# Twenty attention pairs' state and score products: from whole-array and bf16-split products to fp32 quarters in two PSUM banks

## The chip, the cores and the metric

The kernel runs on one core of a Trainium2 chip. The metric is device time in microseconds of one execution, the median over runs; lower is better. TensorE is called PE here, VectorE DVE, ScalarE ACT, GpSimd POOL and SyncE SP, as in the profile.

## The reference, cut to what matters

Three layers follow each other: a linear attention with a per-channel decay, a gated feed-forward layer behind an RMS norm, and a second feed-forward layer with a squared ReLU. The change touches only the first.

```python
# B, H, S, D = 4, 8, 768, 48
for t in range(S):
    cur = einsum('bhd,bhe->bhde', u * k[t], v[t])
    y[t] = einsum('bhd,bhde->bhe', r[t], state + cur)
    state = w[t][..., None] * state + einsum('bhd,bhe->bhde', k[t], v[t])
x = y as (B*S, H*D) = (3072, 384)
x = (silu(xn @ w_gate) * (xn @ w_val)) @ w_out        # xn = x/rms(x)*g, d_ff 1536
out = (s * relu(x @ w_in)**2 + b) @ w_out2            # d_ff 2048
```

## The kernel before, in words

**Attention.** The 768 steps are cut into 6 chunks of 128 steps, and with the 4 batches that gives 24 pairs (`jb` 0 to 23, in the text pairs 1 to 24; `jb // 4` is the chunk, `jb % 4` the batch). `attention(jb, t)` (L322) does one pair for all 8 heads: running products of the decays on DVE (L340, L347), r and k scaled by them (L352, L353), then on PE the scores k against r (`scores`, L383 to L393: 64x64 quarters of each head pair, the two heads p = 0, 1 of a head pair on partitions 0 to 47 and 64 to 111, each into a PSUM bank of its own) with the transposes of k, the copy and causal masking of the scores into the tiles `a` (L410, L411), and then `sums` (L432). `sums` adds into one PSUM bank y what the state gives (L437: 8 products of 112 rows by 64 columns against 96 columns of the state, from pair 5 on, since the first four pairs have no state yet) and what the scores give (L444 or L449), and calls `news` (L454, L457), which makes the increment of the state. An fp32 product of the source stands as two records in the trace, a bf16 or an fp32r one as one.

**Two forms of the score product.** For pairs 1 to 12 (`fine` false) each head is one fp32 product of 128x128 scores against 48 columns of v (L444, 8 products). For pairs 13 to 24 (`FINE = 12`) the scores and v are each split into three bf16 parts (`split_a` L506, `split_v` L516: ACT copies to bf16, DVE or POOL subtracts), and six part products per head run in bf16 (L449, 48 products).

**Room.** PSUM banks 5, 6 and 7 go round among the uses of pairs 5 to 24 (`bank`, L314), in program order: two for the scores, one for the transposes of k, one for y, one for the state's increment, one for the turned x. The bf16 parts of the scores lie in the same room as the tiles `pat` of the weight conversion: `open_fine` (L494) hands the room over after the first layer's weights are converted, `close_fine` (L500) hands it back at the start of the last chunk.

**After sums.** DVE adds u's part, `av`, to y into `ys` (L476); ACT and POOL form the norm, PE turns the row block (L532), ACT and DVE split it into fp32r high and low parts (L539, L540), and the feed-forward layers use them.

**Feed-forward layers.** `mm_in` (L607) and `mm_out` (L590 to L592) make three fp32r products of 128x128 against up to 512 columns for each block, in place of a full fp32 one. Weights come as 64-bit words and are converted on DVE, ACT and POOL (L569 to L581).

**Checks.** Behind the attention, at low priority, DVE reads all decays and weights again and tests their range (`check_decay` L711, `check_weight` L721); 64 loads feed them. At the end a flag chooses a slow path, which is not taken here.

**Order.** Each piece of work is an `op` with a due time, engines and a cost. `Plan.issue` (L129) simulates the five engines and writes down each engine's list: an idle engine takes the ready op with the smallest due time. The due time orders and doesn't hold back. The lists are fixed at build time, so on the chip every engine runs its list in order, and a wrong cost shows as a wait at the head of a list. A DMA is an op of SP with the cost `nbytes / 350e3 + 0.06`, and what it feeds is reckoned ready 2.0 us after that (`PASS["sp"]`). While the first feed-forward steps lack work, the plan fills PE with products of zeros (`idle`, L792).

Of the kernel before, what the change touches and what calls it, by code (L numbers as in the profile page):

```python
# [10 lines left out]
F32 = mybir.dt.float32  # L11
# [12 lines left out]
C = 128  # L24
# [28 lines left out]
FINE, EARLY, NU, NM, NZ, LENT = 12, 12, 4, 4, 8, 6  # L53
SIX = (0, 0), (0, 1), (0, 2), (1, 0), (1, 1), (2, 0)
# [46 lines left out]
class Plan:  # L101
# [27 lines left out]
    def issue(self):  # L129
# [14 lines left out]
        while events:  # L144
# [12 lines left out]
            for e, queue in ready.items():  # L157
                while queue and free[e] <= now:
# [46 lines left out]
def body(ctx: ExitStack, tc: tile.TileContext, rkw, nat, w1, w2, cst, out):  # L205
# [16 lines left out]
    RAW, PAT, SA = [None] * 2, [None] * 2, [None] * 2  # L222
    SV, = tiles(1, "sv", [128, 3, H, D], BF16)
# [55 lines left out]
    def split_room(fine):  # L279
        for i in range(2):  # L280
            if fine:
                SA[i] = sb.tile([128, 3, HP, C], BF16, name=f"sa{i}", tag=f"small{i}")
            else:
                RAW[i] = sb.tile([128, 2 * DM], I64, name=f"raw{i}", tag=f"big{i}")
                PAT[i] = sb.tile([128, 2 * DM], U32, name=f"pat{i}", tag=f"small{i}")

    split_room(False)

# [33 lines left out]
    def attention(jb, t):  # L322
# [36 lines left out]
        fine = jb >= FINE  # L359
# [63 lines left out]
        if fine:  # L423
            split_a(t, A)
            split_v(td, v, n, q)

        i = bank(jb)
        y = PS[i][:, 0:DM].rearrange("p (h d) -> p h d", h=H)
        iu = None if last else bank(jb)
        U = None if last else PS[iu][:RW, 0:HP * D].rearrange("p (h d) -> p h d", h=HP)  # L430

        def sums(e):  # L432
            first = True
            if jb >= B:
                for h in range(HP):
                    for c0 in (0, 64):
                        nc.tensor.matmul(y[c0:c0 + 64, 2 * h:2 * h + 2, :], r[:, h, c0:c0 + 64], ST[b][:, h],  # L437
                                         start=h == 0, stop=False, skip_group_check=True)
                first = False
            for p in range(2):  # L440
                for h in range(HP):
                    end = p == 1 and h == HP - 1
                    if not fine:
                        nc.tensor.matmul(y[:, 2 * h + p, :], AT[A[p]][:, h, :], v[:, 2 * h + p, :],  # L444
                                         start=first, stop=end, skip_group_check=True)
                        first = False
                    else:
# [16 lines left out]
        reads = [(n, p, x) for n in ("sa", "sv") for p in range(2) for x in range(3)] if fine else [("a", s) for s in A]  # L464
        if jb < NU:
            op(t, {"pe": 1.8 + 0.9 * (jb >= B)}, sums, reads + [("v", q)] + [("r", q), ("st", b, 0), ("st", b, 1)] * (jb >= B),
               [("ps", i)])
# [25 lines left out]

    def open_fine(t):  # L494
        keys = [(n, i) for n in ("raw", "pat") for i in range(2)]
        keys += [("sa", i, x) for i in range(2) for x in range(3)]

        op(t, {"pool": 0.0}, lambda e: split_room(True), (), keys, False)

    def close_fine(t):  # L500
        keys = [(n, i) for n in ("raw", "pat") for i in range(2)]
        keys += [("sa", i, x) for i in range(2) for x in range(3)]
        op(t, {"pool": 0.0}, lambda e: split_room(False), (), keys, False)


    def split_a(t, A):  # L506
        for p in range(2):
            s, N = A[p], HP * C
            for x in range(2):
                op(t, {"act": act(N)}, lambda e, s=s, x=x, p=p: nc.scalar.activation(  # L510
                    SA[p][:, x], AT[s], AF.Copy), [("a", s)], [("sa", p, x)])
                op(t, {"dve": vec2(N), "pool": gps(N)}, lambda e, s=s, x=x, p=p: E[e].tensor_tensor(
                    SA[p][:, 2] if x else AT[s], AT[s], SA[p][:, x], ALU.subtract),
                    [("sa", p, x)], [("a", s)] + [("sa", p, 2)] * x)

    def split_v(t, v, n, q):  # L516
        rest, src = n[1], v
        for x in range(2):
# [489 lines left out]
```

## Time and profile before

| | us |
|---|---|
| median of 3 runs | 1000.93 (1000.35 to 1003.07) |
| the profiled execution | 1002.0 |
| its span, first to last instruction | 1000.3 |
| PE busy in the span | 982.5 |
| DVE busy | 669.5 |
| ACT busy | 419.1 |
| POOL busy | 207.6 |

"Busy" of PE counts each product from start to end, and products overlap, so a busy PE need not be at its peak; the distance from one block's start to the next block's start says what a block takes. The chain of waits goes back from the last instruction to what released each step, so what lies on it set the end.

### The profile page before, as it was taken

What the parts mean: (1) busy time and instruction counts of PE and PEld (TensorE: products, weight loads), DVE (VectorE), ACT (ScalarE), POOL (GpSimd) and SP (SyncE); (2) the same over time, 40 slices, a digit from 0 to 9 for tenths busy, and PEclk for the clock granted to TensorE, in tenths of its full rate; (3) what the DMA queues carried; (4) which work ended last, traced back from release to release, by engine and by line L of the source; (5) the groups of instructions that cost most, each with busy time, mean ns of one, the idle gap of its engine ahead of it and who ended that gap; (6) DMA issues with size and microseconds to landing.
All of it is one profiled execution on the core that took longest, in us unless ns stands there. A gap on an engine that the chain in (4) does not pass through costs nothing.

```text
span 1000.3 us, 16015 instructions
## 1 busy us (share of the span) xinstructions
PE 982.5 (98%) x6344; PEld 812.8 (81%) x6346; DVE 669.5 (67%) x1111; ACT 419.1 (42%) x861; POOL 207.6 (21%) x255
## 2 busy tenths in 40 slices
PE   8999999999999999999999999999999999999997
PEld 5887998888888888888888888887778888888886
DVE  7998997456665665554589789999993433433432
ACT  4645642344454444454434334343343433433333
POOL 3202300124445454454303431000000000000000
PEclk9999999999999999999999999999999999999998
DMA  8554552122222221121294566676650000000001
GB/s 243 188 165 132 183 181 82 57 74 62 83 75 59 74 76 53 52 75 43 81 278 150 176 205 203 210 240 226 219 191 1 22 11 1 31 1 1 32 1 35
DMA packets 45569, 106.82 MB, mean 107 GB/s; under 512 B 4016, under 2 KB 19632, under 8 KB 45488
## 3 DMA queue, kind: packets, MB, share of 16 engines
q1 hardware_dynamic: 45488, 105.73, 33.4%
q8 instruction: 51, 0.84, 0.3%
q14 instruction: 30, 0.25, 0.1%
HBM read 94.71 MB, written 11.01 MB: 106 GB/s over the span
## 4 chain that ended last, share of the span: by engine, by line
PE 83%; DVE 9%; DMA 4%; ACT 3%; issue 1%; SPq 0%; ACTq 0%; DVEq 0%
PE b L607 43%; PE b L590 10%; PE b L591 10%; PE b L592 10%; DMA raw<-in_w 3%; PE b L389 2%; PE b L449 2%; PE b L444 1%; PE b L437 1%; PE b L393 1%; PE b L457 1%; DMA out_t<-o 1%; DVE pat L575 1%; DVE hl L681 1%; DVE pat L741 1%
## 5 line engine op out<-in xcount | busy, mean ns | idle before, releaser
L607 PE MATMUL b<-xh,w 128*128 128x512 f32 (+1 forms) x1566 | 486.3, 375 | 1.0 <-DVE sg L303 0.8
L607 PEld LDWEIGHTS b<-xh,w 128*128 128x128 f32 x1566 | 287.8, 188 | 54.2 <-DVE sg L303 1.4
L607 PE MATMUL b<-xl,w 128*128 128x512 f32 (+1 forms) x783 | 292.0, 373 | 0.5 <-DVE xl L540 0.5
L590 PE MATMUL b<-hh,w 128*128 128x512 f32 (+1 forms) x537 | 206.4, 384 | 1.9 <-ACT in L642 0.7
L591 PE MATMUL b<-hl,w 128*128 128x512 f32 (+1 forms) x537 | 203.4, 379 | 1.4 <-DVE hl L681 1.1
L592 PE MATMUL b<-hh,w 128*128 128x512 f32 (+1 forms) x537 | 202.4, 377 | 0.0
L306 ACT ACTIVATE sg<-b 128x512 f32<-128x512 f32 (+1 forms) x179 | 102.0, 570 | 222.7 <-PE b L607 221.2
L607 PEld LDWEIGHTS b<-xl,w 128*128 128x128 f32 x783 | 147.7, 189 | 26.0 <-DVE xl L540 0.7
L678 DVE SCALAR_TENSOR_TENSOR sg<-sg,cs,b 128x512 f32<-128x512 f32 (+1 forms) x97 | 71.8, 740 | 99.2 <-ACT sg L306 98.9
L590 PEld LDWEIGHTS b<-hh,w 128*128 128x128 f32 x537 | 101.1, 188 | 21.9 <-ACT hh L306 1.3
L591 PEld LDWEIGHTS b<-hl,w 128*128 128x128 f32 x537 | 101.2, 188 | 21.2 <-DVE hl L681 2.9
L592 PEld LDWEIGHTS b<-hh,w 128*128 128x128 f32 x537 | 101.1, 188 | 18.3
L306 ACT ACTIVATE hh<-sg,cs 128x512 fp32r<-128x512 f32 (+1 forms) x97 | 69.7, 719 | 88.2 <-DVE sg L678 82.7
L681 DVE SCALAR_TENSOR_TENSOR hl<-sg,cs,hh 128x512 fp32r<-128x512 f32 (+1 forms) x97 | 73.0, 752 | 48.8 <-ACT hh L306 48.8
L306 ACT ACTIVATE hh<-sg 128x512 fp32r<-128x512 f32 (+1 forms) x82 | 47.5, 579 | 110.4 <-DVE sg L303 110.1
L303 DVE TENSOR_TENSOR sg<-b,sg 128x512 f32<-128x512 f32 (+1 forms) x82 | 51.1, 623 | 50.7 <-PE b L607 49.2
L303 DVE TENSOR_TENSOR hl<-sg,hh 128x512 fp32r<-128x512 f32 (+1 forms) x82 | 54.1, 660 | 13.9 <-ACT hh L306 13.6
L581 POOL TENSOR_TENSOR w<-pat,w 128x384 fp32r<-128x384 f32 x28 | 34.2, 1238 | 67.7 <-ACT w L579 64.8
L411 POOL TENSOR_SCALAR_AFFINE_SELECT a<-a 128x512 f32<-128x512 f32 x38 | 29.9, 807 | 78.9 <-ACT a L306 78.9
L579 ACT ACTIVATE w<-pat 128x384 fp32r<-128x384 f32 x68 | 33.1, 520 | 30.0 <-DVE pat L575 27.9
L573 DVE SCALAR_TENSOR_TENSOR pat<-raw,pat 128x768 uint32<-128x768 uint32 (+1 forms) x40 | 36.8, 925 | 0.0
L540 DVE SCALAR_TENSOR_TENSOR xl<-b,cs,xh 128x128 fp32r<-128x128 f32 x72 | 20.8, 344 | 22.4 <-ACT xh L306 22.4
(132 smaller groups left out, 1005.8 us busy)
## 6 DMA issues: line engine op xcount, KB each, us to landing
raw<-in_w SPq DMA_DIRECT2D x56, 768.0 KB, 4.6
in<-in_rkw SPq DMA_DIRECT2D x24, 448.0 KB, 4.5
raw<-in_w SPq DMA_DIRECT2D x24, 384.0 KB, 3.6
n<-in_nat SPq DMA_DIRECT2D x18, 384.0 KB, 3.2
in<-in_rkw SPq DMA_DIRECT2D x24, 226.6 KB, 2.6
x2d<-o SPq DMA_DIRECT2D x21, 256.0 KB, 2.5
a<-in_rkw SPq DMA_DIRECT2D x24, 224.0 KB, 3.7
v<-in_nat SPq DMA_DIRECT2D x24, 192.0 KB, 3.5
```

What stands on the lines that cost most here:

```text
L303: op(when, {e: cost[e] for e in engines}, lambda e: E[e].tensor_tensor(dst, a, b, f), reads, writes, port)
L306: op(when, {"act": act(n)}, lambda e: nc.scalar.activation(dst, src, func, **kw), reads, writes)
L411: op(t, {"pool": 0.60}, lambda e, s=A[p]: nc.gpsimd.affine_select(out=AT[s], in_=AT[s], compare_op=ALU.is_gt, fill=0.0, base=0, pattern=[[ ...
L573: op(t, {"dve": vec2(N)}, lambda e, word=word, pat=pat: nc.vector.scalar_tensor_tensor(pat(), word(1), 0xC0000000, pat(), ALU.bitwise_and, ...
L579: op(t, {"act": act(DM)}, lambda e, c=c, s=s, pat=pat: nc.scalar.activation(W[s][:, 0], pat(c).bitcast(F32), AF.Copy), [("pat", pi)], [("w ...
L581: op(t, {"dve": vec2(DM)} if ph == 0 else {"dve": vec2(DM), "pool": gps(DM)}, lambda e, c=c, s=s, pat=pat: E[e].tensor_tensor(W[s][:, 1], ...
L590: nc.tensor.matmul(dst, wt[:, 0, cols], xh, start=first, stop=False, skip_group_check=True)
L591: nc.tensor.matmul(dst, wt[:, 0, cols], xl, start=False, stop=False, skip_group_check=True)
L592: nc.tensor.matmul(dst, wt[:, 1, cols], xh, start=False, stop=last, skip_group_check=True)
L607: nc.tensor.matmul(dst, W[s][:, w, kk * 128:(kk + 1) * 128], xx[x][:, kk, sl], start=first and j == kk == 0, stop=last and kk == KD - 1 an ...
L678: op(t, {"dve": vec2(n)}, lambda e: nc.vector.scalar_tensor_tensor(sg, sg, s_col, p, ALU.mult, ALU.mult), [("ps", i)], [("sg", q)], False)
L681: op(t, {"dve": vec2(n)}, lambda e: nc.vector.scalar_tensor_tensor(hl, sg, b_col, hh.bitcast(F32), ALU.add, ALU.subtract), [("sg", q), ("h ...
```

## The change

For pairs 5 to 24 the products of state and scores are made in fp32 on quarters of the array (64 rows by 64 columns), what the two row halves give going into two PSUM banks, Y[0] and Y[1]. The state product becomes 16 products of 48 rows by 64 columns against 48 columns, and the score product 32 products of 64 by 64 against 48 columns. A second add on DVE, of the second bank, follows the first. The bf16 splits, their tiles and the handing over of their room go; pairs 1 to 4 keep their form. The plan's cost for `sums` is now 1.5 and 0.6 us. It also reckons at least 0.47 us for a DMA on SP, and 6 us more for the landing of the checks' loads.

```diff
-FINE, EARLY, NU, NM, NZ, LENT = 12, 12, 4, 4, 8, 6
-SIX = (0, 0), (0, 1), (0, 2), (1, 0), (1, 1), (2, 0)
+EARLY, NU, NM, NZ, LENT = 12, 4, 4, 8, 6
...
@@ Plan.issue
-                        begin[k] = max(begin[k], free[e] + self.PASS[e])
+                        begin[k] = max(begin[k], free[e] + self.PASS[e] + (self.ops[i][3] if e == "sp" else 0.0))
...
-    RAW, PAT, SA = [None] * 2, [None] * 2, [None] * 2
-    SV, = tiles(1, "sv", [128, 3, H, D], BF16)
+    RAW, PAT = tiles(2, "raw", [128, 2 * DM], I64), tiles(2, "pat", [128, 2 * DM], U32)
+    zero, = tiles(1, "zero", [128, NB], BF16)
...
-    def dma(when, dst, src, nbytes, reads=(), writes=()):
-        op(when, {"sp": nbytes / 350e3 + 0.06}, lambda e: nc.sync.dma_start(
-            out=dst() if callable(dst) else dst, in_=src), reads, writes)
+    def dma(when, dst, src, nbytes, reads=(), writes=(), land=0.0):
+        op(when, {"sp": max(0.47, nbytes / 350e3 + 0.06)}, lambda e: nc.sync.dma_start(
+            out=dst, in_=src), reads, writes, land)
...
@@ attention
-        if fine:
-            split_a(t, A)
-            split_v(td, v, n, q)
-
-        i = bank(jb)
-        y = PS[i][:, 0:DM].rearrange("p (h d) -> p h d", h=H)
+        iy = [bank(jb) for _ in range(1 + (jb >= B))]
+        i = iy[0]
+        Y = [PS[i][:, 0:DM].rearrange("p (h d) -> p h d", h=H) for i in iy]
         iu = None if last else bank(jb)
         U = None if last else PS[iu][:RW, 0:HP * D].rearrange("p (h d) -> p h d", h=HP)
 
+        def quarters(e):
+            for h in range(HP):
+                for c0 in (0, 64):
+                    for p in range(2):
+                        nc.tensor.matmul(Y[p][c0:c0 + 64, 2 * h + p, :], r[64 * p:64 * p + D, h, c0:c0 + 64],
+                                         ST[b][64 * p:64 * p + D, h, p, :], start=h == 0, stop=False,
+                                         skip_group_check=True)
+            for j in range(H):
+                h, p = divmod(j, 2)
+                for c0 in (0, 64):
+                    for z in range(2):
+                        rows = slice(64 * z, 64 * z + 64)
+                        nc.tensor.matmul(Y[z][c0:c0 + 64, j, :], AT[A[p]][rows, h, c0:c0 + 64], v[rows, j, :],
+                                         start=False, stop=j == H - 1, skip_group_check=True)
+
         def sums(e):
-            first = True
             if jb >= B:
-                for h in range(HP):
-                    for c0 in (0, 64):
-                        nc.tensor.matmul(y[c0:c0 + 64, 2 * h:2 * h + 2, :], r[:, h, c0:c0 + 64], ST[b][:, h],
-                                         start=h == 0, stop=False, skip_group_check=True)
-                first = False
-            for p in range(2):
-                for h in range(HP):
-                    end = p == 1 and h == HP - 1
-                    if not fine:
-                        nc.tensor.matmul(y[:, 2 * h + p, :], AT[A[p]][:, h, :], v[:, 2 * h + p, :],
-                                         start=first, stop=end, skip_group_check=True)
-                        first = False
-                    else:
-                        for x, z in SIX:
-                            nc.tensor.matmul(y[:, 2 * h + p, :], SA[p][:, x, h, :], SV[:, z, 2 * h + p, :],
-                                             start=False, stop=end and x == 2, skip_group_check=True)
+                quarters(e)
+            else:
...
-            op(t, {"pe": (1.3 if fine else 1.8) + 0.9 + 0.6 * (not last)}, sums,
+            op(t, {"pe": 1.5 + 0.6 * (not last)}, sums,
                reads + [("r", q), ("v", q), ("st", b, 0), ("st", b, 1)] + [tk] * (not last),
-               [("ps", i)] + ([] if last else [("ps", iu)]))
+               [("ps", i) for i in iy] + ([] if last else [("ps", iu)]))
             ys, yk = YS[q], ("ys", q)
-            tt(t, DVE, DM, ys, PS[i][:, 0:DM], AV[q].rearrange("p h d -> p (h d)"), ALU.add,
-               [("ps", i), ("av", q)], [yk])
+            tt(t, DVE, DM, ys, PS[iy[0]][:, 0:DM], AV[q].rearrange("p h d -> p (h d)"), ALU.add,
+               [("ps", iy[0]), ("av", q)], [yk])
+            tt(t, DVE, DM, ys, PS[iy[1]][:, 0:DM], ys, ALU.add, [("ps", iy[1])], [yk])
...
-    def open_fine(t):
...
-    def close_fine(t):
...
-    def split_a(t, A):
...
-    def split_v(t, v, n, q):
...
@@ check_decay
-        dma(t, w, rkw[jb, :, 0:HP * WL].rearrange("p (h t) -> p h t", h=HP)[:, :, 1:], RW * HP * C * 4, (), [("a", s)])
+        dma(t, w, rkw[jb, :, 0:HP * WL].rearrange("p (h t) -> p h t", h=HP)[:, :, 1:], RW * HP * C * 4, (), [("a", s)], 6.0)
...
@@ check_weight
-        dma(t, raw, (w1, w2)[ph][f, :, o * DM:o * DM + n], 128 * n * 8, (), [("raw", ri)])
+        dma(t, raw, (w1, w2)[ph][f, :, o * DM:o * DM + n], 128 * n * 8, (), [("raw", ri)], 6.0)
...
-    later(beg[0, 1] + 7 * 5.5, open_fine, beg[0, 1] + 7 * 5.5)
...
-    later(last, close_fine, last)
```

Left out of the diff are the bodies of the functions that go, the lines of pairs 1 to 4, and a few in which `raw` and `pat` are named directly instead of by a function.

## Rows read from the trace of the kernel before

**Rows 1.** Page: busy time and share of the span, instructions; the granted clock in 40 slices.
```profile
PE 982.5 (98%) x6344; PEld 812.8 (81%) x6346; DVE 669.5 (67%) x1111; ACT 419.1 (42%) x861; POOL 207.6 (21%) x255
...
PEclk9999999999999999999999999999999999999998
```

**Rows 2.** Page: chain that ended last, shares by engine.
```profile
PE 83%; DVE 9%; DMA 4%; ACT 3%; issue 1%; SPq 0%; ACTq 0%; DVEq 0%
```

**Rows 3.** Chain in order of time, 60 to 152 us: start, length, what.
```profile
59.71 0.33 DVE sg L303
...
76.39 0.56 DVE ys L303
...
91.48 0.53 DVE ys L303
...
108.21 0.46 DVE ys L303
...
120.09 0.81 PE b L437 x16
120.91 1.92 PE b L444 x16
...
134.91 0.34 DVE sg L303
...
135.30 2.42 PE b L607 x18
```

**Rows 4.** Stretches of 25 us: busy (x instructions) by engine, clock, DMA share, GB/s.
```profile
150.00:175.00 25.00, 25.00 (x119) 20.95 (x118) 17.81 (x32) 7.12 (x14) 1.25 (x3) 1.00 0.27 82
...
500.00:525.00 25.00, 25.00 (x167) 20.68 (x166) 21.37 (x36) 8.09 (x17) 1.59 (x2) 1.00 0.94 276
...
625.00:650.00 25.00, 25.00 (x112) 20.70 (x111) 24.86 (x52) 7.53 (x12) 0.00 (x0) 1.00 0.65 212
...
675.00:700.00 25.00, 24.47 (x107) 19.60 (x106) 24.31 (x47) 7.37 (x12) 0.00 (x0) 1.00 0.66 228
700.00:725.00 25.00, 24.29 (x106) 19.56 (x105) 23.51 (x41) 7.78 (x12) 0.00 (x0) 1.00 0.65 218
725.00:750.00 25.00, 24.66 (x108) 19.86 (x108) 23.27 (x45) 10.72 (x18) 0.00 (x0) 1.00 0.53 193
```

**Rows 5.** Waits, 660 to 760 us: who waited for whom: us, times, longest.
```profile
DVE pat L733 <- DMA raw<-in_w: 3.5, 3, 1.5
...
PE b L591 <- DVE hl L681: 1.1, 3, 0.5
```

**Rows 6.** Timeline of PE, pair 12: start, us, what (records in a row merged).
```profile
233.33 0.88 PE L437 MATMUL b<-st,in 112*64 112x96 f32 x16
234.14 1.99 PE L444 MATMUL b<-v,a 128*128 128x48 f32 x16
236.05 0.67 PE L457 MATMUL b<-v,kt 128*64 128x48 f32 x16
236.65 0.51 PE L590 MATMUL b<-hh,w 128*128 128x512 f32 x1
```

**Rows 7.** Timeline of PE, pair 15, a pair with bf16 splits.
```profile
291.50 0.39 PE L590 MATMUL b<-hh,w 128*128 128x512 f32 x1
...
293.54 0.39 PE L607 MATMUL b<-xh,w 128*128 128x512 f32 x1
...
295.67 0.88 PE L437 MATMUL b<-st,in 112*64 112x96 f32 x16
296.48 1.37 PE L449 MATMUL b<-sv,sa 128*128 128x48 bf16 x48
297.78 0.67 PE L457 MATMUL b<-v,kt 128*64 128x48 f32 x16
298.38 0.50 PE L590 MATMUL b<-hh,w 128*128 128x512 f32 x1
```

**Rows 8.** Timeline of PE, the quartered scores of pair 15.
```profile
285.89 1.10 PE L389 MATMUL b<-in 48*64 48x128 f32 x32
286.92 0.60 PE L393 MATMUL b<-cs,in 112*128 112x112 f32 x4
```

**Rows 9.** Line L389 alone in a stretch of 30 ns: PE and PEld busy (x records).
```profile
285.89:285.92 0.03, 0.03 (x4) 0.03 (x4) 1.00 0.00 0
```

**Rows 10.** Groups by line and shape: busy us, mean ns, idle before.
```profile
L510 ACT ACTIVATE sa<-a 128x512 bf16<-128x512 f32 x48 | 28.9, 632 | 6.9 <-POOL a L411 3.6 <-POOL a L512 1.9 <-DVE a L512 1.0
...
L303 DVE TENSOR_TENSOR ys<-b,av 128x384 f32<-128x384 f32 x20 | 11.1, 555 | 19.6 <-PE b L449 16.7 <-PE b L444 2.3 <-ACT av L376 0.5
```

More of the change, by code (lines that the diff above doesn't have):

```diff
@@ L277, in body @@
     planned = [True]
-    def split_room(fine):
-        for i in range(2):
-            if fine:
-                SA[i] = sb.tile([128, 3, HP, C], BF16, name=f"sa{i}", tag=f"small{i}")
-            else:
-                RAW[i] = sb.tile([128, 2 * DM], I64, name=f"raw{i}", tag=f"big{i}")
-                PAT[i] = sb.tile([128, 2 * DM], U32, name=f"pat{i}", tag=f"small{i}")
-    split_room(False)
     def op(when, engines, fn, reads=(), writes=(), port=True):
@@ L358, in attention @@
         td = t + TD
-        fine = jb >= FINE
         i2 = [bank(jb), bank(jb)]
@@ L432, in sums @@
         def sums(e):
-            first = True
             if jb >= B:
-                for h in range(HP):
-                    for c0 in (0, 64):
-                        nc.tensor.matmul(y[c0:c0 + 64, 2 * h:2 * h + 2, :], r[:, h, c0:c0 + 64], ST[b][:, h],
-                                         start=h == 0, stop=False, skip_group_check=True)
-                first = False
-            for p in range(2):
-                for h in range(HP):
-                    end = p == 1 and h == HP - 1
-                    if not fine:
-                        nc.tensor.matmul(y[:, 2 * h + p, :], AT[A[p]][:, h, :], v[:, 2 * h + p, :],
-                                         start=first, stop=end, skip_group_check=True)
-                        first = False
-                    else:
-                        for x, z in SIX:
-                            nc.tensor.matmul(y[:, 2 * h + p, :], SA[p][:, x, h, :], SV[:, z, 2 * h + p, :],
-                                             start=False, stop=end and x == 2, skip_group_check=True)
+                quarters(e)
+            else:
+                for j in range(H):
+                    p, h = divmod(j, HP)
+                    nc.tensor.matmul(Y[0][:, 2 * h + p, :], AT[A[p]][:, h, :], v[:, 2 * h + p, :],
+                                     start=j == 0, stop=j == H - 1, skip_group_check=True)
@@ L462, in more @@
                              skip_group_check=True)
-        reads = [(n, p, x) for n in ("sa", "sv") for p in range(2) for x in range(3)] if fine else [("a", s) for s in A]
+        reads = [("a", s) for s in A]
         if jb < NU:
-            op(t, {"pe": 1.8 + 0.9 * (jb >= B)}, sums, reads + [("v", q)] + [("r", q), ("st", b, 0), ("st", b, 1)] * (jb >= B),
-               [("ps", i)])
+            op(t, {"pe": 1.8}, sums, reads + [("v", q)], [("ps", i)])
             op(t, {"pe": 0.7}, more, [("av", q), "cs"], [("ps", i)])
@@ L492, in attention @@
         cp(t, DM + 170, xg, ys, [yk, ("rs", q)], [xk], scale=rs[:, 0:1])
-    def open_fine(t):
-        keys = [(n, i) for n in ("raw", "pat") for i in range(2)]
-        keys += [("sa", i, x) for i in range(2) for x in range(3)]
-        op(t, {"pool": 0.0}, lambda e: split_room(True), (), keys, False)
-    def close_fine(t):
-        keys = [(n, i) for n in ("raw", "pat") for i in range(2)]
-        keys += [("sa", i, x) for i in range(2) for x in range(3)]
-        op(t, {"pool": 0.0}, lambda e: split_room(False), (), keys, False)
-    def split_a(t, A):
[L507 to L514, printed above, removed]
-    def split_v(t, v, n, q):
-        rest, src = n[1], v
-        for x in range(2):
-            keys = [("sv", p, x) for p in range(2)]
-            cp(t, DM, SV[:, x], src, [("v", q), ("n", 0)], keys)
-            tt(t, BOTH, DM, SV[:, 2] if x else rest, src, SV[:, x], ALU.subtract,
-               keys + [("v", q)], [("n", 0)] + [("sv", p, 2) for p in range(2)] * x)
-            src = rest
     def attention_x(jb, t):
@@ L549, in weights @@
             N = n * DM
-            def raw(ri=ri, N=N):
-                return RAW[ri][:, 0:N]
+            raw = RAW[ri][:, 0:N]
             def word(i, raw=raw):
-                return raw().bitcast(U32).rearrange("p (n two) -> p n two", two=2)[:, :, i]
+                return raw.bitcast(U32).rearrange("p (n two) -> p n two", two=2)[:, :, i]
             def pat(c=slice(0, N), pi=pi):
@@ L767, in start @@
         dma(60, cs[:, CU:], cst[:, CU:], 128 * DM * 4, (), ["cu"])
-        zero = SV.rearrange("p a h d -> p (a h d)")[:, 0:NB]
         def consts(e):
```

12 lines of the change are left out of this document (4 added, 8 removed).

## The prediction

> **What bounds the kernel now.** I read the page's busy times first: PE 98% of the span, DVE 67%, at a granted clock of nine tenths or more in every slice but the last [rows 1]. That a busy PE is also what sets the end is for the chain of waits to say: PE holds 83% of it, DVE 9%, DMA 4% [rows 2]. The next view is the chain in order of time, to see where the other engines hold it. From 59.7 to 111 us it runs on DVE in the main, from there to 127 us on PE, then on DVE again up to the product "sg" at 134.91, and from 135.30 on PE [rows 3]. The stretches of 25 us agree: from 150 to 675 us PE's column is full, with one product after the other, each 227 ns behind the last (nine between 291.50 and 293.54 [rows 7]), and between 675 and 750 us it shows 107, 106 and 108 products where a full stretch has 112 [rows 4]. So time taken from PE counts where PE holds the chain: nearly all of it after 135 us, none of it while DVE holds it.
>
> **The products, from 135 us on.** Pairs 9 to 24 lie there. A block's price is the distance from its start to the start of the next block. In pair 12, the old form without splits, the state takes 234.14 - 233.33 = 0.81 us and the scores 236.05 - 234.14 = 1.91, together 2.72 [rows 6]. In pair 15, with splits, it is 0.81 and 1.30, together 2.11 [rows 7].
>
> The new block has 16 state and 32 score products, each two records: 96 records, 24 for each quarter of the array. No such block stands in the trace, but three of its kind do. Each of them sends 8 records through its slowest part: the increment (L457, weights 64 wide) takes 298.38 - 297.78 = 0.60 us [rows 7], the state (96 columns) 0.81, the quartered scores (the quarters with 128 columns) 286.92 - 285.89 = 1.03 [rows 8]. From one to the next a column costs 0.21 / (8 x 32) = 0.82 and 0.22 / (8 x 32) = 0.86 ns, say 0.84, and a fixed 0.60 - 8 x 64 x 0.84 = 0.17 us is left. The new records stream 48 columns but load 64, so I count 64: 24 x 64 x 0.84 = 1.29, plus 0.17 = 1.46 us. The old scores, 16 records of 128, come to 1.72 by this and took 1.91, so the fixed part grows by about 0.02 to 0.03 per 8 records; for 16 more I add 0.06 and take **1.52 us**. As the upper end all of L457's time is put on its records, 0.60 / 8 x 24 = 1.80. All this needs four quarters at work at once. The quartered scores show it: four of their records are at work within 30 ns of the first start [rows 9].
>
> Pairs 9 to 12 save 4 x (2.72 - 1.52) = 4.8 us, pairs 13 to 24 save 12 x (2.11 - 1.52) = 7.1, together **11.9 us**; with 1.46 it is 12.8, with 1.80 it is 7.4.
>
> **Pairs 5 to 8.** They lie around 76 to 123 us, where DVE holds the chain at the add into ys of pairs 5, 6 and 7 (76.39, 91.48, 108.21) and PE at pair 8 (120.09) [rows 3]. The second add puts another DVE instruction there, 0.555 us by the mean of the first [rows 10]; on the chain the first adds hold 0.56, 0.53 and 0.46, so three more are +1.5. Pair 8's products give back 1.20. Net I take **+0.3 us**. Ends: four adds and no gain, +2.2; all four blocks gained as later ones are, -4.8.
>
> **Second adds and banks of later pairs.** The add of pairs 9 to 24 costs nothing on the path: DVE is busy 17.8 of 25 us at 150 us [rows 4], and what it feeds is due a chunk later. If that cover were gone, each would cost 0.5 us. The seventh claim on three banks makes the next pair's scores wait for readers that are through long before, pairs being (295.67 - 233.33) / 3 = 21 us apart on PE [rows 6, 7]. Price nothing.
>
> **Splits removed.** 48 ACT copies of 632 ns [rows 10], and as many subtractions on DVE and POOL, go; they ran beside a full PE, so their going frees engines and no time. What is late next there is still PE. The two hand-overs of room cost POOL nothing; without them the second layer's weights can be loaded before the last chunk starts. The stretch 500 to 525, with DMA at 0.94, had a full PE anyway [rows 4]: nothing.
>
> **Costs in the plan.** Only order can change by them. The floor of 0.47 us for a DMA touches a few small ones. The 6 us more for the checks' loads move DVE's check instructions back in its list. Today DVE waits at its head for such a load (L733, 3.5 us in three waits), while "hl", which PE needs, is queued behind it; L591 waits for that [rows 5]. SP's own list holds the same 64 loads, and nothing that PE needs waits on it there. The most to be had is the 3 x 112 - 321 = 15 products missing, 15 x 0.227 = 3.4 us [rows 4]; as lower end a re-drawn list loses as much. I take **-2.0**, between the 1.1 that PE shows as waits for hl alone and 3.4.
>
> **Sum.** -11.9 + 0.3 - 2.0 = -13.6 us. Against the profiled execution, 1002.0, it gives 988.4; the median of the runs is 1.1 lower, so **987.3 us**. With all ends: 1000.9 - 12.8 - 4.8 - 3.4 = 979.9, and 1000.9 - 7.4 + 2.2 + 3.4 = 999.1; the upper ends are unlikely to meet, so 996.
>
> **A rule against it.** The bf16 block starts its 48 records at 1.30 / 48 = 27 ns each [rows 7]; the new block needs 16 ns. The Trainium skill, "TensorE: Matmul & The Clock Gate", section "Wait — 56ns, not 53.3ns?", says that starts never come closer than about 25 ns, however few the columns. Taken for the whole array, an estimate from it is 96 x 25 = 2.4 us for a block, and the sum would be 12 x 0.29 - 4 x 0.32 = +2.2 us in place of -11.9. The four records within 30 ns [rows 9] speak against it across quarters.
>
> **Rivals.** (1) Pace of issue: 96 records can't follow each other faster than the bf16 ones do. For it: no block of the trace keeps up 16 ns for long. Against it: rows 9. At 27 ns a block takes 2.60 us: 12 x 0.49 - 4 x 0.12 = +5.4, and with +0.3 and -2.0 the time is 1004.6, slower. It decides from 23.5 ns a record on, where a block takes (4 x 2.72 + 12 x 2.11) / 16 = 2.26 us. (2) The change doesn't do what it says, the two row halves taking turns: 48 x 64 x 0.84 + 0.17 = 2.75 us a block, +7.8, 1007. Against it: the scores' four quarters took 1.03 us, the time of one quarter's 8 records. (3) The head pays as well: PE has other work at hand while DVE is late, and pairs 5 to 8 give up to 4.8 us: 982. Against it: the chain's DVE stretches. (4) DVE's crowded stretch takes it back. From 600 to 750 us DVE is nearly full, and PE comes to it 12 us earlier. If each of the ten stretches from 500 to 750 lost what the worst one loses (6 products, 1.4 us), it is 13.6 lost in place of 3.4: 1000.9 - 11.9 + 0.3 + 10.2 = 999.5, no change; half of it is 993. Against it: the checks can go on into 750 us and later.
>
> **How the numbers follow.** The forecast 0.62, (3) 0.13, (4) 0.13 of which 0.05 near no change, (1) 0.08, (2) 0.04. Less than 0.3%, 3 us, is about what a measurement can't tell from no change. Faster: 0.62 + 0.13 + 0.08 and a little of (1), 0.84; same 0.06; slower 0.10. The range 980 to 996 holds the forecast, (3) and half of (4), and leaves out (1), (2) and the rest of (4), 0.17.
>
> **What would show it.** Right: from the state's first record to the increment's (L457) some 1.5 us in every pair from 5 on, 96 records, no L449, no splits; PE full from about 135 us; the whole chain from there moved up by 12 us at 525; 112 products in the stretches that had 107, 106 and 108. Wrong: a block above 2.2 us (rivals 1, 2); the block short but PE's stretches with gaps (4); a second add of ys on the chain after 150 us; the head shorter than before (3).

## The result, and the profile after

The changed kernel takes 990.77 us (median of 4 runs, 989.73 to 992.74), the kernel before 1001.17 in the same comparison (4 runs, 1000.35 to 1003.07). The ratio is 0.9896, with a 95% interval of 0.9873 to 0.9919: 10.4 us less. That is faster, as forecast, inside the range, and 3.5 us above the 987.3 forecast. The profiled execution took 989.75 us, with a span of 988.0.

The page of the changed kernel: busy time by engine, and the chain that ended last, by engine.

```profile
PE 967.2 (98%) x7242; PEld 800.9 (81%) x7242; DVE 644.0 (65%) x1084; ACT 379.5 (38%) x789; POOL 173.3 (18%) x230
...
PE 89%; DVE 5%; ACT 2%; DMA 2%; issue 1%; POOL 0%; DVEq 0%; ACTq 0%; POOLq 0%
```

PE is busy for 15.3 us less than before [rows 1], though it has 898 records more. Its share of the chain rose from 83% to 89%, DVE's fell from 9% to 5% [rows 2]. The next view is the timeline of PE at pair 9 (start, us, what; records in a row merged), the counterpart of [rows 6] and [rows 7].

```profile
178.87 0.68 PE L421 MATMUL b<-st,in 48*64 48x48 f32 x32
179.37 1.11 PE L429 MATMUL b<-v,a 64*64 64x48 f32 x64
180.42 0.67 PE L446 MATMUL b<-v,kt 128*64 128x48 f32 x16
181.01 0.50 PE L547 MATMUL b<-hh,w 128*128 128x512 f32 x1
```

L421 are the state's quarters, L429 the scores', L446 the increment. From the state's first record to the increment's is 180.42 - 178.87 = 1.55 us, where the old block took 2.72 or, with splits, 2.11. In the last four pairs there is no increment, and the old block took less, as the timeline of PE before the change shows at pair 21:

```profile
434.97 0.88 PE L437 MATMUL b<-st,in 112*64 112x96 f32 x16
435.78 1.37 PE L449 MATMUL b<-sv,sa 128*128 128x48 bf16 x48
437.00 0.48 PE L590 MATMUL b<-hh,w 128*128 128x512 f32 x1
```

That is 437.00 - 434.97 = 2.03 us. The sixteen blocks of pairs 9 to 24 give 4 x 1.17 + 8 x 0.56 + 4 x 0.48 = 11.1 us, or 11.2 with the durations unrounded. The stretches show what became of it (busy and count of PE, PEld, DVE, ACT, POOL, then clock, DMA share, GB/s; the last line is a closer look at 10 us).

```profile
75.00:100.00 25.00, 19.17 (x244) 15.49 (x244) 21.39 (x36) 13.41 (x43) 9.36 (x14) 0.93 0.46 129
...
150.00:175.00 25.00, 25.00 (x129) 21.39 (x128) 23.93 (x41) 7.83 (x16) 1.01 (x3) 1.00 0.60 179
...
200.00:225.00 25.00, 25.00 (x335) 20.39 (x326) 17.44 (x32) 9.75 (x23) 10.33 (x16) 1.00 0.31 90
...
575.00:600.00 25.00, 24.31 (x106) 19.49 (x105) 22.37 (x28) 12.29 (x24) 10.49 (x9) 1.00 0.65 216
...
650.00:675.00 25.00, 24.77 (x109) 20.14 (x108) 18.08 (x34) 10.50 (x17) 0.00 (x0) 1.00 0.57 180
675.00:700.00 25.00, 25.00 (x112) 20.68 (x112) 17.77 (x33) 8.11 (x13) 0.00 (x0) 1.00 0.38 115
700.00:725.00 25.00, 25.00 (x112) 20.72 (x111) 18.39 (x32) 10.82 (x19) 0.00 (x0) 1.00 0.40 139
725.00:750.00 25.00, 25.00 (x112) 20.72 (x111) 17.54 (x29) 8.42 (x13) 0.00 (x0) 1.00 0.42 146
...
95.00:105.00 10.00, 6.79 (x55) 5.83 (x56) 8.88 (x16) 6.40 (x20) 2.87 (x5) 0.66 0.31 85
```

The three stretches from 675 to 750 us, which had 107, 106 and 108 products [rows 4], are full with 112. Gaps stand at 575 us (106 products) and at 650 us (109), where the kernel before had none; it had one at 525 us instead (109 products). And in the head the granted clock fell to a mean of 0.66 between 95 and 105 us, partly at the lower level of 1.2 GHz; before, it was full in all these slices [rows 1].

**Milestones.** To see where the time went, I use a count that all kernels share: the products with 256 or 512 columns are the same 3,960 in each and stand in the same order of pairs, with the others between them. The table gives the start of no. 700 (just ahead of pair 9's block), of no. 2000 (behind all of the changed blocks) and of no. 3000 (most of the checks are done), worked out from one profiled execution each; the count starts at 0, and the products of zeros are left out. The first line is in us, the others are differences from it; the names of the experiments are explained below.

```
kernel                       no. 700   no. 2000  no. 3000
before                        175.68     548.01    778.36
changed                        +2.64     -10.40    -12.20
changed, again                 +3.64      -9.23    -11.18
e1 from pair 9                 +0.14     -11.14    -13.10
e1, again                      -0.48     -11.84    -13.67
e2 checks as before            +3.56      -8.81     -8.09
e3 before, checks later        +1.19      +1.46     -0.46
e4 row halves                  +5.62      +5.63      +3.81
e6 old cost in the head        +4.14      -8.83    -10.54
e7 no second add in the head   -0.24     -13.26    -14.95
e8 av on POOL                  +6.35      -9.03    -10.70
e9 av on PE                    +2.02     -10.72    -12.58
e10 both adds together         -0.51     -10.73    -12.52
```

The order in which the list puts the wide products between the small ones of the head differs a little from kernel to kernel, so the first column is only a guide to the head. I take the head from the second: what a kernel has at no. 2000 beyond the 11.2 us of the sixteen later blocks. By that the changed kernel's head (pairs 5 to 8) cost 11.2 - 10.4 = 0.8 us in one execution and 11.2 - 9.2 = 2.0 in another. The same program thus differs by about 1 us here, and e3, in which DVE, ACT and POOL have the lists of before up to 450 us, stands 1.2 us off at no. 700. So differences of a microsecond between two single executions say little.

### The profile page after: what moved, and what is told of

The parts are those of the page before. It is cut to its first block, busy times and chain, and to the rows that moved or that the text cites. A ratio compares the mean times of both kernels' runs of the same rounds, so it can differ in the third digit from the quotient of the medians.

```text
span 988.0 us, 17701 instructions
## 1 busy us (share of the span) xinstructions
PE 967.2 (98%) x7242; PEld 800.9 (81%) x7242; DVE 644.0 (65%) x1084; ACT 379.5 (38%) x789; POOL 173.3 (18%) x230
## 4 chain that ended last, share of the span: by engine, by line
PE 89%; DVE 5%; ACT 2%; DMA 2%; issue 1%; POOL 0%; DVEq 0%; ACTq 0%; POOLq 0%
PE b L564 47%; PE b L547 11%; PE b L548 11%; PE b L549 11%; PE b L377 2%; PE b L429 2%; PE b L421 1%; PE b L381 1%; PE b L446 1%; DMA raw<-in_w 1%; PE b L490 1%; DVE pat L532 1%; DVE pat L530 1%; PE b L744 1%; DVE w L538 1%
## 5 line engine op out<-in xcount | busy, mean ns | idle before, releaser
L538 POOL TENSOR_TENSOR w<-pat,w 128x384 fp32r<-128x384 f32 x30 | 39.8, 1346 | 65.8 <-ACT w L536 65.8
L292 POOL TENSOR_TENSOR st<-st,pm 64x192 f32<-64x192 f32 (+1 forms) x37 | 22.3, 604 | 78.7 <-DVE st L292 59.6
L292 DVE TENSOR_TENSOR ys<-b,av 128x384 f32<-128x384 f32 x20 | 11.1, 555 | 38.2 <-PE b L429 37.7
```

Source lines behind the costliest of these rows:

```text
L292: op(when, {e: cost[e] for e in engines}, lambda e: E[e].tensor_tensor(dst, a, b, f), reads, writes, port)
L538: op(t, {"dve": vec2(DM)} if ph == 0 else {"dve": vec2(DM), "pool": gps(DM)}, lambda e, c=c, s=s, pat=pat: E[e].tensor_tensor(W[s][:, 1], ...
```

## The experiments

**The quarters: row halves apart (e4).** Are four quarters at work at once, or does something else make the block short? The same 96 records in another order: all of the first row half, then all of the second, for the state and for the scores.

```diff
-            for h in range(HP):
-                for c0 in (0, 64):
-                    for p in range(2):
+            for p in range(2):
+                for h in range(HP):
+                    for c0 in (0, 64):
...
-            for j in range(H):
-                h, p = divmod(j, 2)
-                for c0 in (0, 64):
-                    for z in range(2):
+            for z in range(2):
+                for j in range(H):
+                    h, p = divmod(j, 2)
+                    for c0 in (0, 64):
```

> The changed kernel with the same 48 products in another order: all of the first row half, then all of the second, for the state and for the scores. The sums are the same, and so are the plan and its costs. Theory A (the block is short because four quarters work at once): only two work at once now, and a block goes from 1.55 to 2.9 us or so (48 records behind each other in a column half, at 58 ns), 16 blocks after 135 us cost 16 x 1.35 = 22 us more, about 1012. Rival B (the block is bound by the pace of issue, 96 records at 16 ns): the order of issue changes nothing, about 991.

Measured: 1006.47 us (1005.74 to 1016.51), ratio 1.0064 [1.0034, 1.0093]. The timeline of PE of e4 in one block:

```profile
293.21 0.77 PE L421 MATMUL b<-st,in 48*64 48x48 f32 x26
293.77 0.26 PE L429 MATMUL b<-v,a 64*64 64x48 f32 x2
293.82 0.22 PE L421 MATMUL b<-st,in 48*64 48x48 f32 x2
...
293.98 1.67 PE L429 MATMUL b<-v,a 64*64 64x48 f32 x58
295.59 0.67 PE L446 MATMUL b<-v,kt 128*64 128x48 f32 x16
```

The block takes 295.59 - 293.21 = 2.38 us in place of 1.55 with nothing changed but the order, though not Theory A's 2.9, so the gain does come from four quarters at work together, and a mere pace of issue, which would not care for the order, is out. (Each row half has a PSUM bank of its own, so the run doesn't tell the row halves from their banks.) Single records of the two traces show it too: in the changed kernel they start in fours, 5 to 8 ns apart, a four every 58 ns; in e4 they start in twos, a two every 58 ns. The block is shorter than two halves strictly in turn would be, 48 x 58 ns = 2.8 us, and the lines above show why: scores of the first row half (L429, 293.77) start ahead of state records of the second (L421, 293.82) that stand before them in the program. The halves overtake each other, and this shortens the block.

**What a quarter's record costs (e5).** The new records stream 48 columns and load 64; the forecast counted the 64. Here only columns 0 to 23 of each head are computed: half of y is left out.

```diff
-                        nc.tensor.matmul(Y[p][c0:c0 + 64, 2 * h + p, :], r[64 * p:64 * p + D, h, c0:c0 + 64],
-                                         ST[b][64 * p:64 * p + D, h, p, :], start=h == 0, stop=False,
+                        nc.tensor.matmul(Y[p][c0:c0 + 64, 2 * h + p, 0:24], r[64 * p:64 * p + D, h, c0:c0 + 64],
+                                         ST[b][64 * p:64 * p + D, h, p, 0:24], start=h == 0, stop=False,
...
```

(and the scores' products in the same way).

> The changed kernel with the quarter products against 24 columns of state and v in place of 48; half of y is left out. The plan and the number of products are the same. Theory A (a quarter's record takes 58 ns because 64 weight columns are loaded for it): the block stays at 1.55 us. Rival B (the 48 streamed columns set it): the block falls to 1.0 to 1.2 us.

Measured: 997.46 us in a single run; its first wide product starts 6.8 us later than in the kernel before, so its total can't be compared, but the block can:

```profile
186.98 0.66 PE L421 MATMUL b<-st,in 48*64 48x24 f32 x32
187.47 1.11 PE L429 MATMUL b<-v,a 64*64 64x24 f32 x64
188.51 0.67 PE L446 MATMUL b<-v,kt 128*64 128x48 f32 x16
```

188.51 - 186.98 = 1.53 us with half the columns, against 1.55. What streams doesn't set the time of such a block. A load of 64 columns fits: the old scores, which stream the same 48 columns but load 128, took 1.91 us for 16 records [rows 6], 0.12 us each, about twice the 58 ns of a quarter's record. No run changed the load alone.

**The head without the change (e1).** Pairs 5 to 8 keep the old products, the old cost in the plan, one bank and one add.

```diff
-        iy = [bank(jb) for _ in range(1 + (jb >= B))]
+        iy = [bank(jb) for _ in range(1 + (jb >= 2 * B))]
...
-            if jb >= B:
+            if jb >= 2 * B:
                 quarters(e)
             else:
+                if jb >= B:
...
-            op(t, {"pe": 1.5 + 0.6 * (not last)}, sums,
+            op(t, {"pe": (1.5 if jb >= 2 * B else 2.7) + 0.6 * (not last)}, sums,
...
-            tt(t, DVE, DM, ys, PS[iy[1]][:, 0:DM], ys, ALU.add, [("ps", iy[1])], [yk])
+            if jb >= 2 * B:
+                tt(t, DVE, DM, ys, PS[iy[1]][:, 0:DM], ys, ALU.add, [("ps", iy[1])], [yk])
```

> Pairs 5 to 8 keep the old products in one bank, with their old cost in the plan and without the second add; pairs 9 to 24 are as in the changed kernel. Theory A (the list redrawn around pairs 5 to 8, not the blocks themselves, cost the head 2.6 us, in a 3.7 us wait of PE before the turned block of pair 6 and the half clock after it): the wait goes back to about 1 us, the clock stays full up to 150 us, and the time is 2 to 3 us below the changed kernel, about 988. Rival B (the head's loss has another source, such as the DMA floor in the plan's costs): the wait stays, and the old blocks cost up to 4.7 us more, 991 to 995.

Measured: 989.09 us (988.85 to 989.38), ratio 0.9869 [0.9839, 0.9900], 1.7 below the changed kernel, less than the 2 to 3 expected; the wait and the clock are as Theory A has them (0.9 us, full). Both kernels were then measured side by side:

> The changed kernel once more, as it is, beside the other two on one chip: 989.5 to 993 by its earlier runs.

> The kernel with old products in pairs 5 to 8 and quarters from pair 9 on, once more beside the changed one. Theory (the new form in pairs 5 to 8 takes back about 1 us of what the later pairs give): 1 to 2 us below the changed kernel of the same call. Rival (the difference of the first call was the chip's): within 0.5 us of it.

They gave 990.93 (990.82 to 991.73) for the changed kernel and 989.06 (988.32 to 996.61) for e1. With the old head the kernel is 1.9 us faster: in pairs 5 to 8 the change costs time. At no. 2000 e1 stands at -11.1 and -11.8, which is the 11.2 of the sixteen later blocks within the spread.

**What in the head costs it.** The waits of the changed kernel between 60 and 150 us (who waited for whom: us, times, longest):

```profile
ACT l L295 <- DVE ys L292: 4.9, 1, 4.9
...
PE b L490 <- ACT l L295: 4.1, 2, 3.5
...
ACT xg L295 <- POOL rs L470: 2.2, 1, 2.2
...
PE b L490 <- ACT xg L295: 1.3, 1, 1.3
```

and its DVE and POOL in the same place:

```profile
76.11 0.56 DVE L292 TENSOR_TENSOR ys<-b,av 128x384 f32<-128x384 f32 x1 [0.32 <-ACT av L364]
76.58 1.22 DVE L329 TENSOR_TENSOR_SCAN l<-in,ones 112x516 f32<-112x516 f32 x1
77.72 0.53 DVE L292 TENSOR_TENSOR ys<-b,ys 128x384 f32<-128x384 f32 x1
...
78.77 0.63 DVE L292 TENSOR_TENSOR in<-in,l 112x512 f32<-112x512 f32 x1
79.31 1.22 DVE L336 TENSOR_TENSOR_SCAN l<-in,rg 112x516 f32<-112x516 f32 x1
80.45 0.53 DVE L292 TENSOR_TENSOR l<-l 128x384 f32<-128x384 f32 x1
80.90 0.69 DVE L292 TENSOR_TENSOR in<-in,l 112x512 f32<-112x512 f32 x1
```

```profile
79.31 2.08 POOL L470 TENSOR_TENSOR rs<-rs,col 128x1 f32<-128x1 f32 x1 [0.66 <-ACT rs L295]
...
88.55 2.04 POOL L399 TENSOR_SCALAR_AFFINE_SELECT a<-a 128x512 f32<-128x512 f32 x1 [0.78 <-ACT a L295]
90.55 1.55 POOL L399 TENSOR_SCALAR_AFFINE_SELECT l<-l 128x512 f32<-128x512 f32 x1
```

The two adds of pair 5 start 77.72 - 76.11 = 1.61 us apart, since the list has put a scan of the next pair between them. What waits for them then meets a slow POOL: one number for each partition (L470) takes 2.08 us, and the masks of the next scores 2.04 and 1.55. PE waits 3.5 us in one place for the normed rows (L490), and its clock falls behind that. The changed kernel's chain in order of time, in part, shows what of this set the pace:

```profile
74.16 1.54 ACT av L364 x7
...
79.31 2.09 POOL rs L470
...
93.31 0.55 DVE ys L292
...
94.26 0.47 DVE ys L292
...
95.74 1.91 ACT av L364 x8
```

Of the four second adds only that of pair 6 (94.26) lies on it; in pair 5 it runs through POOL's step. Five runs try these things.

**The cost in the plan (e6):** pairs 5 to 8 get their old 2.7 back, with the new products.

```diff
-            op(t, {"pe": 1.5 + 0.6 * (not last)}, sums,
+            op(t, {"pe": (1.5 if jb >= 2 * B else 2.7) + 0.6 * (not last)}, sums,
```

> The changed kernel, pairs 5 to 8 also with new products and second adds, but with the old cost of their sums (2.7 and 0.6 us) in the plan. Theory A1 (the shorter cost in the plan redrew the lists of the head): the wait before the turned block of pair 6 goes back to 1 to 1.5 us, the clock stays full, about 988.5. Theory A2 (the second adds did it): the wait of more than 3 us and the dip of the clock stay, 990 to 992.

Measured: 991.80 us (991.46 to 992.41), ratio 0.9895 [0.9856, 0.9934]: no better. The time and a wait of 3.3 us are Theory A2's, but not its clock, which between 95 and 105 us stayed full (PEclk is the third number from the end, in the stretches of e6):

```profile
95.00:105.00 10.00, 6.27 (x65) 5.16 (x66) 8.25 (x17) 7.50 (x23) 2.64 (x4) 1.00 0.46 147
```

Its DVE at the adds of pair 5, and its POOL:

```profile
76.23 0.56 DVE L292 TENSOR_TENSOR ys<-b,av 128x384 f32<-128x384 f32 x1 [0.51 <-ACT av L364]
76.71 0.34 DVE L292 TENSOR_TENSOR st<-b,st 64x192 f32<-64x192 f32 x1
76.97 0.54 DVE L292 TENSOR_TENSOR ys<-b,ys 128x384 f32<-128x384 f32 x1
```

```profile
78.66 0.88 POOL L470 TENSOR_TENSOR rs<-rs,col 128x1 f32<-128x1 f32 x1
```

Here no scan stands between the two adds of pair 5 (they start 0.74 us apart), and POOL's step takes 0.88 us. The head is no shorter for it.

**No second add (e7):** the second bank's part of y is left out for pairs 5 to 8.

```diff
-            tt(t, DVE, DM, ys, PS[iy[1]][:, 0:DM], ys, ALU.add, [("ps", iy[1])], [yk])
+            if jb >= 2 * B:
+                tt(t, DVE, DM, ys, PS[iy[1]][:, 0:DM], ys, ALU.add, [("ps", iy[1])], [yk])
```

> The changed kernel without the second add of pairs 5 to 8 (the second bank's part of y is left out for them). Theory A2 (the second adds made the head late): the wait before the turned block of pair 6 falls to about 1 us, the clock stays full, about 988. Theory A1 (the shorter cost of the blocks in the plan did it): the wait and the dip stay, 990 to 992.

Measured: 988.20 us (987.07 to 995.45), ratio 0.9881 [0.9835, 0.9928]. That is 2.6 and 2.7 below the two medians of the changed kernel, which was not measured beside it. At no. 2000 it stands at -13.3, against -10.4 and -9.2 with the adds, 2.9 to 4.0 us; but its profiled execution, 987.07, is its fastest, 1.1 below its median. Four of the adds' own durations are 4 x 0.54 = 2.2. What the new products of pairs 5 to 8 give by themselves comes to 0.9 by the medians (against e1's 989.1), and to 13.3 - 11.2 = 2.1 by no. 2000. A wait and the stretch of e7:

```profile
PE b L491 <- DVE in L292: 5.0, 1, 5.0
```

```profile
95.00:105.00 10.00, 7.76 (x66) 6.42 (x66) 9.14 (x17) 6.82 (x20) 1.93 (x3) 0.70 0.38 113
```

The time is Theory A2's, but its signs, a short wait and a full clock, didn't come: PE waits for 5.0 us, with a mean clock of 0.70 behind it, and the head is still short, while in e6 the clock was full and the head long. So neither PE's longest wait nor its clock tells how long the head is. That DVE sets the pace in the head is one reading; e9 below tries it.

**Both adds as one piece of the plan (e10):** nothing can come between them.

```diff
-            tt(t, DVE, DM, ys, PS[iy[0]][:, 0:DM], AV[q].rearrange("p h d -> p (h d)"), ALU.add,
-               [("ps", iy[0]), ("av", q)], [yk])
-            tt(t, DVE, DM, ys, PS[iy[1]][:, 0:DM], ys, ALU.add, [("ps", iy[1])], [yk])
+            def both(e):
+                nc.vector.tensor_tensor(ys, PS[iy[0]][:, 0:DM], AV[q].rearrange("p h d -> p (h d)"), ALU.add)
+                nc.vector.tensor_tensor(ys, PS[iy[1]][:, 0:DM], ys, ALU.add)
+
+            op(t, {"dve": 2 * vec2(DM)}, both, [("ps", iy[0]), ("ps", iy[1]), ("av", q)], [yk], False)
```

> The changed kernel with the two adds of each of pairs 5 to 24 as one piece of work in the plan, so that no other DVE instruction stands between them. The sums are the same. Theory A3 (in the head the second add costs more than its own 0.5 us because the list puts a scan of 1.2 us between it and the first, for pair 5, and what then stands on POOL at the same time takes 2 us instead of 0.6): the second add of pair 5 starts about 0.5 us after the first, the head is 1 to 1.5 us shorter, 989 to 990. Rival (the adds' own time on a full DVE is the cost, wherever they stand): no difference beyond 0.5 us, 990.5 to 991.5.

Measured: 989.86 us (989.34 to 996.96), ratio 0.9891 [0.9856, 0.9927], as Theory A3 has it, and 0.9 and 1.1 below the two medians of the changed kernel, which was not measured beside it. At no. 2000 it stands at -10.7, against -10.4 and -9.2, so a gain of 1 us is not clear of what one kernel differs by from execution to execution. With e6, where the scan was gone as well and the head stayed long, the scan is not shown to be the cause. The adds now follow each other, and POOL's small step is shorter (timelines of DVE and of POOL of e10):

```profile
75.67 0.56 DVE L465 TENSOR_TENSOR ys<-b,av 128x384 f32<-128x384 f32 x1 [0.33 <-ACT av L364]
76.26 0.56 DVE L466 TENSOR_TENSOR ys<-b,ys 128x384 f32<-128x384 f32 x1
```

```profile
78.28 0.87 POOL L472 TENSOR_TENSOR rs<-rs,col 128x1 f32<-128x1 f32 x1 [3.03 <-ACT rs L295]
```

**The other work beside them (e8, e9).** In the changed kernel ACT scales v head by head ahead of the first add (L364, eight copies of 1.9 us together). In e8 POOL does that in one instruction; in e9 PE adds that part through the identity, ACT copies the second bank out, and DVE has one add again in pairs 5 to 8.

```diff
-            if jb < NZ:
-                def scaled(e):
...
-                op(td, {"act": 8 * act(D)}, scaled, [("ac", q), ("v", q)], [("av", q)])
...
+            tt(td, POOL if jb < NZ else DVE if jb < EARLY else BOTH, DM, AV[q], v, AC[q].to_broadcast([128, H, D]), ALU.mult,
```

```diff
+            if jb < 2 * B:
+                op(t, {"pe": 0.7}, more, [("av", q), "cs"], [("ps", i)])
+                cp(t, DM, ys, PS[iy[1]][:, 0:DM], [("ps", iy[1])], [yk])
+                tt(t, DVE, DM, ys, PS[i][:, 0:DM], ys, ALU.add, [("ps", i)], [yk])
+            else:
...
```

> The changed kernel with u's part of pairs 5 to 8 scaled in one POOL instruction in place of eight on ACT. Theory A (the 3.5 us wait of PE hangs on ACT, where eight copies of 1.9 us stand ahead of the scaling that PE waits for): the wait falls to 1 to 2 us, the clock stays full, and the time is 1.5 to 3 us below the changed kernel, 987.5 to 989. Rival B (POOL is the late one, with masks of 1.5 to 2 us beside DVE): POOL's instruction makes the mask and the norm later still, and the time is as the changed kernel's or above, 991 to 993.

> The changed kernel, but for pairs 5 to 8 PE adds u's part into the first bank by a product with the identity, ACT copies the second bank out, and DVE has one add as before the change. Theory A2 (in the head DVE sets the pace, and what its second adds take comes on top): the head is as short as without the second adds, 987 to 988.5 in all. Rival B (the chain from the sums to the turned block sets the pace, whichever engine has the step): the copy on ACT and the wait of PE for u's part take the place of the add, 990 to 992.

Measured: e8 993.13 us (990.91 to 1002.10), ratio 0.9922 [0.9892, 0.9952], 2.2 above the repeated changed kernel, which was not measured beside it, and as rival B has it: e8's chain runs through POOL's mask (2.04 us at 88.99) and its step on one number (1.52 us at 96.27). e9 988.93 us (988.67 to 989.36), ratio 0.9878 [0.9851, 0.9905], 2.0 below the changed kernel measured beside it; rival B's 990 to 992 is out. Taking DVE's second add away in pairs 5 to 8 gives about its four durations (2.2 us), even when PE and ACT get more to do.

**The checks' loads (e2, e3).** e2 is the changed kernel with the 6 us taken from the two loads of the checks; e3 is the kernel before with that time alone added.

```diff
-        dma(t, w, rkw[jb, :, 0:HP * WL].rearrange("p (h t) -> p h t", h=HP)[:, :, 1:], RW * HP * C * 4, (), [("a", s)], 6.0)
+        dma(t, w, rkw[jb, :, 0:HP * WL].rearrange("p (h t) -> p h t", h=HP)[:, :, 1:], RW * HP * C * 4, (), [("a", s)])
...
-        dma(t, raw, (w1, w2)[ph][f, :, o * DM:o * DM + n], 128 * n * 8, (), [("raw", ri)], 6.0)
+        dma(t, raw, (w1, w2)[ph][f, :, o * DM:o * DM + n], 128 * n * 8, (), [("raw", ri)])
```

> The changed kernel with the 6 us for the landing of the checks' loads taken out of the plan. Theory A (the later place of the check instructions on DVE gave back some 2 us after 525 us): PE has gaps again in the stretches before 750 us, and the time is 1.5 to 3 us above the changed kernel. Rival B (PE's gaps there go for another reason, such as PE coming earlier): within 0.5 us of the changed kernel.

> The kernel before with nothing but the 6 us for the landing of the checks' loads in its plan. Theory A: the 3.4 us of gaps between 675 and 750 us shrink to about 1 us, 998.5 to 999.5. Rival B: the stretch is short of DVE time whatever the order, and the gaps move elsewhere: 1000.5 to 1001.5.

Measured: e2 994.27 us (992.54 to 1004.77), ratio 0.9929 [0.9897, 0.9961], 3.5 above the changed kernel's 990.77 and 5.2 above e1, which was measured beside it: Theory A, and somewhat more than it expected. Its waits from 550 to 830 us and one of its stretches:

```profile
DVE pat L685 <- DMA raw<-in_w: 3.2, 4, 2.2
...
PE b L547 <- ACT hh L295: 1.0, 1, 1.0
```

```profile
650.00:675.00 25.00, 23.34 (x99) 18.12 (x98) 21.87 (x43) 9.44 (x16) 0.00 (x0) 1.00 0.70 224
```

e3 took 1000.45 us (999.01 to 1006.81), ratio 1.0004 [0.9980, 1.0029], which doesn't tell 2 us from nothing, and is not the 998.5 to 999.5 of Theory A. Its trace tells more: 112 products where there were 107, and, as rival B has it, a new gap at 600 us.

```profile
600.00:625.00 25.00, 23.86 (x104) 19.09 (x103) 24.90 (x36) 12.78 (x22) 6.01 (x5) 1.00 0.61 199
...
675.00:700.00 25.00, 25.00 (x112) 20.71 (x111) 17.28 (x32) 8.41 (x13) 0.00 (x0) 1.00 0.39 121
```

Between no. 2000 and no. 3000 the changed kernel gains 1.8 us (12.20 - 10.40) and 1.95 when repeated, e3 gains 1.9 on the kernel before, and e2 loses 0.7: there PE, coming earlier by the blocks' gain, meets DVE's head waiting for the same loads. The ten stretches from 525 to 775 us say the same: of 10 x 112 products 19 are missing before, 11 in e3, 9 in the changed kernel and 21 in e2, each worth 0.227 us.

## Why the prediction was right, and where it was off

**The blocks of pairs 9 to 24: right.** 1.52 us was forecast from 8 records of 64 loaded columns in each quarter and a fixed part, and 1.55 came; the sum is 11.2 in place of 11.9, since the old blocks of pairs 21 to 24 took 2.03 and not the 2.11 of pair 15. e5 shows that the 48 streamed columns were not the ones to count, e4 that the four quarters are what makes the block short.

**The rule against it, and rival 1 (pace of issue).** The 64 score records start within 180.42 - 179.37 = 1.05 us, which is 16.4 ns from one to the next. What the Trainium skill, "TensorE: Matmul & The Clock Gate", section "Wait — 56ns, not 53.3ns?", says of starts never closer than about 25 ns does not hold across the quarters of this kernel; the measurement decides. Rival 1's 1004.6 us fell with it.

**Rival 2 (row halves in turn)** named a true price for another order: e4 is that order, and its 1006.47 us is near the 1007 that the rival gave. But the block was 2.38 us, not 2.75, since the halves overtake each other; by the milestones the sixteen blocks lose 2.1 us in place of 7.8, the head loses 5.6 - 2.1 = 3.5 in place of 0.3, and the checks give back 1.8. The total is near by luck.

**Pairs 5 to 8: the term that was mis-sized.** "Net I take +0.3 us" was +0.8 in one execution and +2.0 in another, and the medians of the changed kernel and e1, measured side by side, differ by 1.9. The part that was off is the second adds: 1.5 us forecast, 2.0 by e9, 2.6 to 2.7 by e7's median and 2.9 to 4.0 by its milestone. The products' 1.20 lies within what the runs give (0.9 to 2.1). The step that failed was to leave the chain of before as it was and lay three more durations on it. Four adds at 0.54 on a DVE that is nearly full, 2.2 us, are enough for e9's figure, and the prediction had this as its upper end; but the chain itself became another one, with one second add on it (94.26) and POOL's 2.09 us at 79.31. Whether the adds cost more than their own durations stays open. The scan that the list put between the adds of pair 5 was suspected, and e6 speaks against it. Rival 3, a head that pays, is excluded by e1.

**The checks' loads: right.** -2.0 was forecast, -1.8 and -1.95 came, and e3's trace, though not its time, shows it without the rest. The forecast took them as a term of their own, but the runs show that they also guard the other term: without them (e2) the crowded stretch takes 0.7 us back from the blocks' gain. That is rival 4 in a small form. With them, two gaps remain (106 products at 575 us, 109 at 650), and the blocks' gain reaches the end. (The forecast read PE's column before as full from 150 to 675 us; at 525 us 3 products were missing there already.)

**Nothing from splits, banks and later second adds: as forecast.** PE's column is full in every stretch from 150 to 575 us; from 175 to 500 us, where pairs 9 to 24 lie, DVE is busy for 17.44 of 25 us at most, and behind 135 us no add into ys lies on the chain. ACT is busy for 40 us less and POOL for 34 us less over the span [rows 1], and neither shows in the time.

**The rest of the 3.5 us.** In the profiled executions the gain was 1002.0 - 989.75 = 12.3 us against 13.6 forecast: 0.5 from the head, 0.7 from the blocks, 0.2 from the checks. The other 2.1 us are the choice of execution: the prediction took 1.1 off because the profiled execution of before lay above its median, and that of the changed kernel lay 1.0 below its own. The range was wide enough for both.

## What to carry to other kernels

Small fp32 products on four 64x64 quarters run four at a time if the quarters alternate in program order; here a four of 64 loaded columns took 58 ns, whether 24 or 48 columns streamed. With the row halves apart, the sixteen blocks lost 2.1 us instead of gaining 11.2. The second accumulator that this needs is free where the engine that adds it has slack, and costs about its duration or more where that engine is nearly full and near the path (2.0 to 4.0 us here for four adds of 0.54): there keep the old form, as e1 does (989.06), or give the add to an engine that has time, as e9 does (988.93). In a kernel whose order is drawn up by a planner, the time that a load takes to land belongs in the plan. An add's price is better read from the chain after the change than from its duration on the chain before.

## What the runs showed of the hardware that was not expected

POOL's instruction on one number for each partition (L470) took 2.08 us beside DVE's work in pair 5. Its median over the 24 of the changed kernel is 0.55 us, and it took 0.87 in pair 5 of e10, where other DVE work ran beside it. The Trainium skill, "SBUF — State Buffer", section "Who interferes with whom", says that a VectorE instruction with two inputs in SBUF contends with a GpSimd one that reads SBUF. The trace agrees: DVE instructions with both inputs in SBUF run without a break from 78.77 to 81.59 and cover the 2.08 us. All 24 of them fit: in each of the seven that took over 0.8 us, such a DVE instruction was at work when POOL's started, and POOL's ended some 0.4 us after the end of one; when the 17 others started, which took 0.54 to 0.55 us, none was (at 96.03 it was one with an input in PSUM). That they are the cause was not tried by itself.

Records of one row half overtook earlier ones of the other in e4 (a score product at 293.77 ahead of a state product at 293.82), so that two halves in turn took 2.38 us, less than one after the other would.

The clock between 95 and 105 us fell to a mean of 0.66 in the changed head and of 0.70 in e7, where PE waited 3.5 and 5.0 us; in e6, with a wait of 3.3 us further on (until 132.28), it stayed full throughout the head. The head with the longest of these waits was the shortest, so the dip alone does not decide; what it costs was not measured.
